# Two turned loads of w2 placed one unit earlier in the first pass of a fused backward kernel

## The chip, the cores and the metric

The kernel runs on one core of one Trainium2 chip, as one program. The metric is the device time of one execution in microseconds (us); lower is better. A profiled execution gives the trace: every instruction with its engine, line, start and duration, the DMA packets, and who released whom. TensorE (PE) multiplies matrices, with its weight loads shown apart (PEld), VectorE is DVE, ScalarE is ACT, GpSimd is POOL and SyncE is SP; the last two mostly issue DMAs here.

## The reference

The reference computes a gated sum of two branches and all its gradients. Cut to what matters:

```python
def forward(x, w_r, w_i, w1, b1, w2, b2, gate_w, B_x):    # x: 1 x 2048 x 1024
    g = sigmoid((x * gate_w).sum(-1, keepdims=True))
    a = irfft2(rfft2(x) * (w_r + 1j * w_i))               # spectral branch
    h = relu(x @ w1 + b1) ** 2                            # w1: 1024 x 3584
    b = h @ w2 + b2                                       # w2: 3584 x 1024
    return g * a + (1 - g) * b

out, vjp = jax.vjp(forward, ...)
return out, *vjp(grad_out)      # gradients of x, w_r, w_i, w1, b1, w2, b2, gate_w
```

`x` is the argument `A_x`; both branches read it. Inputs and outputs are bfloat16.

## The kernel before, in words

The work has three passes over the dense branch, with the spectral branch (the "side") dealt into their gaps.

The first pass, `mlp_in`, makes the hidden layer and its gradient. The 3584 hidden columns are 28 chunks of 128, taken in 14 pairs `fp`; two pairs make one of seven groups `fg` of 512 columns, the first being group 0. After a start over pairs 0 and 1, the pass is a list of units `(fp, sp)`, where `sp` is a half of the 2048 rows: (2,0), (2,1), (3,0), (3,1), (4,0), (4,1) and so on up to pair 10, then five more in another order. A unit makes the hidden layer of its pair and half with seven products (`p1` to `p7`, matmuls of L876, each a chain of four of 512 columns) and, in between, the four gradient products of the unit before it (`back_(waiting[0..3])`, matmuls of L776, chains of eight), each closed by a VectorE instruction (L780) that writes `dhT`; `later["last"]` is the newest of these. A unit takes some 16 us.

The gradient products read `w2T`, a group of w2 turned by the DMA itself: `load_w2(fg)` issues two transposing DMAs on SyncE (L183 is the helper), each of 256 rows of w2, half a megabyte. The tile `w2T` has two buffers, so group `fg + 1` is written over group `fg - 1`. A unit's gradient products belong to the unit before it, so the last products of group `fg - 1` run in the first unit of group `fg`. The load is tied to `later["last"]`: SyncE waits for that instruction before it issues.

Also on SyncE are the loads of w1 (`w1g`, L798, half a megabyte for each pair, two buffers), which `load_w1(fp + 1)` asks for at the start of a pair's first unit. The side's first stage, `first_stage`, takes 16 pairs of row tiles `src`, eight of x and then eight of the incoming gradient. GpSimd issues their loads (L707) from the fourth pair on, into three buffers; VectorE folds each pair (`uv`, L273 and L274, then L278 to L285), ScalarE copies edges of the folds (L280 to L286), TensorE transforms them (L294, L326), and GpSimd stores the result to `z_scr` (L240).

The order of instructions on each engine is chosen by a planner, which goes by the order of the text where it can, by expected durations, and by explicit ties: `after(...)` with its default is a real wait, with `NoSync` an order on one engine only. Each engine then runs its own list strictly in order. The same holds for SyncE and GpSimd as issuers of DMAs.

Of the kernel before, what the change touches and what calls it, by code (L numbers as in the profile page):

```python
# [141 lines left out]
def kernel(  # L142
# [35 lines left out]
    FGW, FG, FGC = g.FGW, g.FG, g.FGC  # L178
# [557 lines left out]
    def mlp_in():  # L736
# [48 lines left out]
        def load_w2(fg, earlier=None):  # L785

            w2T[fg] = wb.tile([P, DC, FGW], BF16, name="w2T", tag="w2T", bufs=2)
            for h in (0, FGW // 2):
                f0 = fg * FGW + h
                after(turned(w2T[fg][:, :, h : h + FGW // 2], B_w2[f0 : f0 + FGW // 2, :]), earlier)  # L790
# [5 lines left out]
        def load_w1(fp):  # L796
            w1[fp] = f1.tile([P, DC, PW], BF16, name="w1f", tag="w1f") if fp == 2 else wb.tile([P, DC, PW], BF16, name="w1g", tag="w1g", bufs=2)
            ld(out=w1[fp][:], in_=w1v[:, :, fp * PW : (fp + 1) * PW])  # L798
# [27 lines left out]
        def back_(fp, s, c):  # L826
            if (fp, s // 2) not in dh:
                dh[fp, s // 2], left_of[fp, s // 2] = wide("dhT"), 4
            last = grads(2 * fp + c, s, rows_(s), rTs.pop((fp, s, c)), dh[fp, s // 2][:, c, rows_(s % 2)])
            later["last"] = last  # L830
            left_of[fp, s // 2] -= 1
            if not left_of[fp, s // 2]:
                store(dhT_scr, dh.pop((fp, s // 2)), fp, s // 2)
# [23 lines left out]
        def w_sums(fp, tie=None):  # L857
            (a11, a12), (a21, a22) = w_quads(fp)
            if fp % 2:
                s_ = kept[:, NT - 2 : NT, :].rearrange("p t (n f) -> p (t n) f", f=P).rearrange("p (q n) f -> p q n f", q=4)  # L860
            else:
                s_ = wb.tile([P, 4, KH, P], FP16, name="Sw", tag="Sw", bufs=1)
            s1, s2, s3, s4 = (s_[:, n] for n in range(4))
            for out, x, y, op in ((s1, a21, a22, ALU.add), (s2, s1, a11, ALU.subtract), (s3, a11, a21, ALU.subtract), (s4, a12, s2, ALU.subtract)):
                after(V(out=out, in0=x, in1=y, op=op), later["last"] if tie else None, mybir.DependencyClass.NoSync)
                yield
            S_[fp] = {1: s1, 2: s2, 3: s3, 4: s4}
# [67 lines left out]
        def sum_of_db(n):  # L935
            ec, h = divmod(n, 2)
            summed = nc.vector.reduce_sum(out=gb2[:, ec, h : h + 1], in_=dbT[:, ec, h * S // 2 : (h + 1) * S // 2], axis=mybir.AxisListType.X)
            after(summed, later["last"], mybir.DependencyClass.NoSync)

        def grad_of_b2():  # L940
            whole = wb.tile([P, DC], BF16, name="gb2b", tag="gb2b")
            V(out=whole[:], in0=gb2[:, :, 0], in1=gb2[:, :, 1], op=ALU.add)
            pb = fps.tile([DC, P], BF16, name="pb2", tag="ps2", bufs=2)
            nc.tensor.transpose(pb[:], whole[:], identb[:])
            row = wb.tile([DC, P], BF16, name="gb2r", tag="gb2r")
            nc.vector.tensor_copy(out=row[:], in_=pb[:])
            st(out=out_7.rearrange("(c p) -> c p", p=P), in_=row[:])
# [27 lines left out]
        def freed_rows(n, low, high):  # L975
            if n == freed + 1:
                again(slice(2 * low, 2 * low + 2), later["last"])
            elif n == len(seq) - 1 and high:
                again(slice(6 + 2 * high, 8 + 2 * high))
# [4 lines left out]
        for n, u in enumerate(units_):  # L984
            fg, pr = divmod(u.fp, NPR)
            if (u.fp, u.sp) == (LAST - 2, 1):
                load_w1(LAST)
            elif u.sp == 0 and u.fp < LAST - 1:
                load_w1(u.fp + 1)
            u.p1()  # L990
            if n:
                units_[n - 1].square(0, u.copy)
            back_(*waiting[0])
            u.p5()
            freed_rows(n, 0, 1)
            if first and u.sp and "mid" in later and u.fp >= FC // 4:
                turned_group(0, *first.pop(0), later["last"])
            yield
            next(more_sums, None)
            u.p6()  # L1000
            freed_rows(n, 1, 2)
            if n:
                units_[n - 1].square(1, u.copy)
            back_(*waiting[1])
            next(more_sums, None)
            follows = u.fp + 1 if u.sp == 1 and u.fp < LAST - 2 else {(LAST - 2, 0): LAST - 1, (LAST - 1, 1): LAST}.get((u.fp, u.sp))
            ahead_ = w_sums(follows, True) if follows else iter(())
            dealt = ahead_ if (u.fp, u.sp) != (LAST - 2, 0) else iter(())
            next(dealt, None)
            yield  # L1010
            u.p7()
            back_(*waiting[2])
            next(more_sums, None)
            next(dealt, None)
            freed_rows(n, 2, 0)
            yield
            back_(*waiting[3])
            for _ in ahead_:
                pass
            next(more_sums, None)  # L1020
            if pr == 0 and u.sp == 0:
                later["blocks"] = later["last"]
            if 0 < fg < FG - 1 and pr == 0 and u.sp:
                load_w2(fg + 1, later["last"])
            if 0 < n <= 2 * DC:
                sum_of_db(n - 1)
            elif n == 2 * DC + 1:
                grad_of_b2()
            u.p4()
            freed_rows(n, 3, 3)  # L1030
            u.p3()
            if n + 1 < len(units_):
                units_[n + 1].p2()
            yield
            waiting = [(u.fp, 2 * u.sp + j, c) for c, j in ((0, 0), (0, 1), (1, 1), (1, 0))]
# [17 lines left out]
    def turned_group(n, i, k, earlier):  # L1053
        scr, fg = (h2T_scr, dhT_scr)[n // FG], n % FG
        rows_ = scr[:].rearrange("c p s -> (c p) s")[fg * FGW + i * FGW // 2 : fg * FGW + (i + 1) * FGW // 2]
        tiles, f_ = slice(k * NT // 2, (k + 1) * NT // 2), slice(i * FGW // 2, (i + 1) * FGW // 2)
        after(turned(group(n)[:, tiles, f_], rows_[:, k * S // 2 : (k + 1) * S // 2]), earlier)
# [699 lines left out]
    warm(7)  # L1757

    units = mlp_in()
    rows_of_x(0)  # L1760
    vrow = f1.tile([FC + DC, P], BF16, name="vrow", tag="vrow")
# [136 lines left out]
```

## Time and profile before

| what | value |
|---|---|
| median of three runs | 1201.8 us (1199.36 to 1203.73) |
| the profiled execution | 1199.23 us, of which span 1197.5 us |
| TensorE busy | 1179.0 us, 98% of the span |
| VectorE, ScalarE, GpSimd busy | 889.6, 533.2, 375.4 us |
| granted TensorE clock | 1.00 |
| DMA moved | 249.84 MB, mean 209 GB/s |
| first pass | from the start to about 460 us |
| w2 groups three to seven, first issue | 110.9, 177.3, 241.1, 303.4 and 364.8 us |

The span runs from the first to the last instruction of the program; the execution's own time has about 1.7 us more around it. Busy time is the union of an engine's instructions. Matmuls are pipelined and their ends are modelled, so a busy TensorE can still lose a little time between starts. An idle stretch is put down to the semaphore that came last.

### The profile page before, as it was taken

To read this page: it belongs to the slowest core of one execution; us is meant where nothing else is said; L and a number is where in the kernel's file an instruction comes from. 1 tells how busy PE (TensorE), PEld (TensorE's weight loads), DVE (VectorE), ACT (ScalarE), POOL (GpSimd) and SP (SyncE) were. 2 spreads that over 40 slices of the span, in tenths; PEclk is the share of its full clock that TensorE was granted. 3 is DMA by queue.
4 is the path that set the end of the run, shared out by engine and by line. 5 is a ranking of instruction groups with operands and counts; after the bars stand their busy time and mean duration, and the time that the engine had idled before them with its cause. 6 is when DMAs were issued, how large, how long until landed. Compare 5 with 4: busy or idle time off the path is not lost.

```text
span 1197.5 us, 19460 instructions
## 1 busy us (share of the span) xinstructions
PE 1179.0 (98%) x7201; PEld 635.5 (53%) x7295; DVE 889.6 (74%) x1593; ACT 533.2 (45%) x959; POOL 375.4 (31%) x618
## 2 busy tenths in 40 slices
PE   9999999999999999999999999999999999999998
PEld 5555555443333444444446899999544444444444
DVE  4898886688988888767638656566786677986757
ACT  4678787576767773444415556554201010000000
POOL 0233443566666663643322322321001100000000
PEclk9999999999999999999999999999999999999999
DMA  9996757796969888989897999995879999665530
GB/s 289 266 309 172 225 168 189 207 223 185 223 177 200 251 242 180 200 188 215 201 225 155 224 226 236 254 202 157 262 184 264 244 276 263 184 190 153 179 124 36
DMA packets 329465, 249.84 MB, mean 209 GB/s; under 512 B 187913, under 2 KB 287659, under 8 KB 328859
## 3 DMA queue, kind: packets, MB, share of 16 engines
q1 hardware_dynamic: 268352, 112.12, 44.0%
q0 software_dynamic: 35136, 111.72, 29.2%
q10 hardware_dynamic: 25882, 24.76, 7.2%
q8 instruction: 57, 0.93, 0.3%
q14 instruction: 38, 0.30, 0.1%
HBM read 114.82 MB, written 89.67 MB: 171 GB/s over the span
## 4 chain that ended last, share of the span: by engine, by line
PE 66%; DVE 10%; ACT 3%; issue 3%; ACTq 0%; POOL 0%; DMA 0%; DVEq 0%; POOLq 0%
PE pX L1194 16%; PE xX L1493 14%; PE pV L1194 12%; PE xV L1493 7%; PE pd L776 5%; PE ph L876 4%; PE xZ L1493 4%; PE pui L326 1%; PE pki L592 1%; PE px L436 1%; DVE rT L892 1%; DVE dhT L780 1%; PE pv L467 1%; DVE tt L447 1%; DVE oT L1441 1%
## 5 line engine op out<-in xcount | busy, mean ns | idle before, releaser
L776 PE MATMUL pd<-dbT,w2T 128*128 128x512 bf16 x861 | 205.8, 379 | 2.2 <-DVE dhT L780 0.4
L776 PEld LDWEIGHTS <-w2T 128*128 128x128 bf16 x896 | 86.5, 98 | 104.1 <-issue 4.3
L1493 PEld LDWEIGHTS <-dS 128*128 128x128 f16 x686 | 66.4, 98 | 78.6 <-issue 3.0
L780 DVE SCALAR_TENSOR_TENSOR dhT<-pd,rT 128x512 bf16<-128x512 f32 x112 | 76.5, 683 | 27.0 <-PE pd L776 23.6
L1544 POOL DMA_DIRECT2D out_dram<-ot x32 | 17.4, 542 | 250.7 <-DVE ot L1600 128.0
L1610 ACT ACTIVATE w2br<-w2br,dsc 128x512 f32<-128x512 bf16 x8 | 5.8, 722 | 175.8 <-DVE ot L1600 117.4
L1210 ACT COPY u<-pX 128x512 f32<-128x512 f32 x56 | 32.8, 585 | 98.7 <-PE pX L1194 93.3
L1493 PE MATMUL xX<-oT,dS 128*128 128x512 f16 x336 | 76.4, 379 | 0.2 <-DVE eR L1522 0.2
L1493 PEld LDWEIGHTS <-odd 128*128 128x128 bf16 (+1 forms) x462 | 44.8, 98 | 51.5 <-issue 0.9
L1493 PEld LDWEIGHTS <-even 128*128 128x128 bf16 (+1 forms) x448 | 43.7, 98 | 52.6 <-issue 0.7
L1194 PEld LDWEIGHTS <-T 128*128 128x128 f16 x672 | 64.7, 98 | 7.8 <-issue 0.7
L893 ACT ACTIVATE rT<-rT 128x512 bf16<-128x512 bf16 x69 | 43.3, 628 | 42.8 <-DVE rT L892 42.8
L761 ACT ACTIVATE h2T<-rT 128x1024 bf16<-128x1024 bf16 x56 | 59.6, 1065 | 0.5 <-issue 0.2
L1214 DVE TENSOR_TENSOR whi<-pV,u 128x512 bf16<-128x512 f32 x28 | 19.3, 688 | 51.6 <-ACT u L1210 51.5
L476 POOL DMA_DIRECT2D y_scr<-pc x64 | 46.9, 734 | 34.1 <-DVE pc L473 31.6
L447 DVE TENSOR_TENSOR tt<-x,w 128x1028 f16<-128x1028 f16 (+1 forms) x64 | 42.0, 690 | 17.1 <-issue 12.6
L1194 PEld LDWEIGHTS <-S 128*128 128x128 f16 x336 | 32.3, 98 | 41.0 <-DVE S L1126 1.3
L1194 PEld LDWEIGHTS <-resL 128*128 128x128 bf16 x448 | 43.0, 98 | 4.7
L1194 PEld LDWEIGHTS <-resR 128*128 128x128 f16 (+1 forms) x448 | 42.9, 98 | 4.9 <-issue 0.2
L807 POOL DMA_DIRECT2D h2T_scr<-h2T x28 | 20.7, 738 | 74.0 <-ACT h2T L761 54.1
L1194 PEld LDWEIGHTS <-even 128*128 128x128 bf16 (+1 forms) x256 | 24.5, 98 | 30.8 <-issue 2.1
L500 POOL DMA_DIRECT2D out_dram<-gw x64 | 34.4, 542 | 19.4 <-ACT gw L496 13.9
(383 smaller groups left out, 2748.3 us busy)
## 6 DMA issues: line engine op xcount, KB each, us to landing
h2T_scr<-h2T POOLq DMA_DIRECT2D x28, 512.0 KB, 4.1
dhT_scr<-dhT POOLq DMA_DIRECT2D x28, 512.0 KB, 4.7
y_scr<-pc POOLq DMA_DIRECT2D x64, 128.0 KB, 3.8
ax_scr<-yo POOLq DMA_DIRECT2D x16, 512.0 KB, 5.0
out_dram<-ot POOLq DMA_DIRECT2D x31, 256.0 KB, 3.4
z<-z_scr ACTq DMA_DIRECT2D x60, 128.0 KB, 4.1
out_dram<-whi POOLq DMA_DIRECT2D x28, 256.0 KB, 5.3
out_dram<-wlo POOLq DMA_DIRECT2D x28, 256.0 KB, 4.7
```

Of the source, the lines that this page charges most:

```text
L447: V(out=tt[:, k, :, :, 0:W], in0=x[:, a : a + 2, :, 0:W], in1=by, op=ALU.mult)
L476: st(out=columns_of(y_scr, c, h), in_=pc[:, n])
L500: st(out=every(dst_w, k), in_=gw[lanes[n], c_, 0:W1])
L761: after(nc.scalar.activation(h2T, rT, ACT.Square), behind_, mybir.DependencyClass.NoSync)
L776: mm(pd[:], lhsT=w_[:, ec, fc % FGC * P : (fc % FGC + 1) * P], rhs=dbT[:, ec, ss], start=(ec == 0), stop=(ec == DC - 1),)
L780: return STT(out=dhT, in0=pd[:], scalar=2.0, in1=rT, op0=ALU.mult, op1=ALU.mult, accum_out=gb1part[:, fc, sb : sb + 1],)
L807: st(out=scr[2 * fp : 2 * fp + 2, :, cols2].rearrange("c p s -> p c s"), in_=t_[:])
L876: mm(acc[:], lhsT=lhs[:, t, :], rhs=rhs[:, t, :], start=start and t == 0, stop=t == KH - 1, skip_group_check=True)
L893: nc.scalar.activation(rT, rT, ACT.Relu)
L1194: self.mm = mm(out, lhsT=lhs[:, t, m * P : (m + 1) * P], rhs=rhs[:, t, :], start=start and t + a == 0, stop=t == KH - 1, skip_group_check= ...
L1210: turn["ACT"] = nc.scalar.copy(out=t_[:], in_=self.X[:])
L1493: ins = mm(acc, lhsT=lhs[:, fc, :], rhs=rhs[:, fc, :], start=start and fc == 0, stop=fc == KH - 1 and bias is None, skip_group_check=True,)
```

## The change

For each group from the second on, the load of the next group is asked for after the last gradient product of the first pair's unit. Before, this was the second unit of that pair (`u.sp` is 1) for all groups. Now it is the first unit (`u.sp` is 0) where `fg` is 1 or 2, so for the loads of the third and fourth group (`load_w2(2)` and `load_w2(3)`), and still the second unit where `fg` is 3, 4 or 5.

```diff
             if pr == 0 and u.sp == 0:
                 later["blocks"] = later["last"]
-            if 0 < fg < FG - 1 and pr == 0 and u.sp:
+            if 0 < fg < FG - 1 and pr == 0 and u.sp == (fg > 2):
                 load_w2(fg + 1, later["last"])
```

In units of the list, the third group's load moves from (2,1) to (2,0), and the fourth's from (4,1) to (4,0). No instruction is added or removed.

## The prediction

> **What bounds the kernel.** I read the page's busy times first, then its chain of work that ended last, then stretches of the first pass, then the queues around the two loads that move.
>
> ```profile
> span 1197.5 us, 19460 instructions
> PE 1179.0 (98%) x7201; PEld 635.5 (53%) x7295; DVE 889.6 (74%) x1593; ACT 533.2 (45%) x959; POOL 375.4 (31%) x618
> PE 66%; DVE 10%; ACT 3%; issue 3%; ACTq 0%; POOL 0%; DMA 0%; DVEq 0%; POOLq 0%
> ```
>
> TensorE (PE) is busy for 1179.0 of 1197.5 us, so all its idle time is 18.5 us, start and end included; the chain that ended last is mostly matmuls, and DMA has 0% of it. An edit that moves loads can only win back idle TensorE time, or add some. Where that lies near the moved loads is seen by stretches (columns: us; PE, PEld, DVE, ACT, POOL busy with counts; granted clock; DMA share; GB/s):
>
> ```profile
> 90.00:107.50 17.50, 17.10 (x117) 9.27 (x117) 15.54 (x32) 14.20 (x30) 7.78 (x14) 1.00 0.48 161
> 107.50:125.00 17.50, 17.28 (x127) 9.90 (x127) 13.78 (x30) 14.43 (x30) 7.09 (x14) 1.00 0.91 225
> 157.50:172.50 15.00, 14.89 (x109) 8.59 (x110) 12.83 (x31) 12.42 (x25) 5.88 (x12) 1.00 0.41 131
> 172.50:190.00 17.50, 17.39 (x120) 9.74 (x121) 14.35 (x32) 15.19 (x32) 6.95 (x14) 1.00 1.00 208
> 190.00:207.50 17.50, 15.97 (x112) 8.83 (x112) 10.39 (x23) 12.81 (x26) 4.52 (x8) 1.00 0.59 176
> ```
>
> The clock is 1.00 throughout. Today's loads fall into 107.5 to 125 (DMA 0.91) and 172.5 to 190 (DMA 1.00); the stretches where they will fall are at 0.48 and 0.41. TensorE idles little except after the second load: 17.50 - 15.97 = 1.53 us in 190 to 207.5. SyncE's queue shows the loads (start, time to issue):
>
> ```profile
> 110.89 9.63 SPq L183 DMA_TRANSPOSE w2T<-in_B_w_dram  x2
> 144.05 0.37 SPq L798 DMA_DIRECT2D w1g<-in_B_w_dram  x1
> 177.31 7.40 SPq L183 DMA_TRANSPOSE w2T<-in_B_w_dram  x2
> 184.82 26.85 SPq L798 DMA_DIRECT2D w1g<-in_B_w_dram  x2
> ```
>
> Why TensorE idles after the second load stands in the time lines of VectorE (DVE), ScalarE (ACT) and TensorE; the bracket is the idle time before the instruction and what ended it:
>
> ```profile
> 191.51 0.48 DVE L723 TENSOR_SCALAR kg<-kf,gcol 128x256 f16<-128x256 f16 x2
> 194.57 0.69 DVE L273 TENSOR_TENSOR uv<-src 128x1024 f16<-128x1024 bf16 x1 [2.58 <-DMA src<-in_grad_out_dram]
> 195.90 0.21 ACT L280 COPY f<-uv 128x4 f16<-128x4 f16 x1 [2.21 <-DVE uv L274]
> 196.73 1.02 PE L876 MATMUL ph<-xT,w1g 128*128 128x512 bf16 x4 [0.68 <-ACT rT L890]
> 200.32 1.02 PE L876 MATMUL ph<-dbn 128*128 128x512 f16 x4 [0.58 <-DVE rT L892]
> ```
>
> The last pair of gradient rows (src) landed late. VectorE, which works in order, stood 2.58 us before the fold that reads it; ScalarE stood behind the fold, with the relu that empties a PSUM bank queued after it; TensorE then wanted that bank. The src pair was issued by GpSimd at 180.56 and 181.14, in the middle of the transposes, and took 11.7 and 13.3 us to land; the same pair issued at 159.7, with no transposes in flight, took 3.0 and 3.8, one issued at 112.7, under the earlier transposes, 7.0.
>
> **The two loads leave their places.** Nothing waits for w2 itself: the idle time before its products is put down to VectorE or the weight load's issue, never to a w2 DMA. Group three is in flight from 110.89 and landed by 123.4, while its first product runs at 163.9; group four's first product runs near 228.5. So 38 us or more are spare already, and a sooner start wins nothing by being sooner. [...]
>
> What is worth something is what they collide with. Leaving 177.3 to about 190 frees the src pair of 180.56: with a delay of 3.0 to 7.0 us it lands by 188.2, and VectorE could start the fold at 191.51 + 0.48 = 191.99. The 2.58 us wait goes whole. For TensorE that is 0.68 + 0.10 + 0.58 + 0.06 = 1.4 us of idle gaps (two more small ones in the same stretch). Modelled ends hide a little: matmuls of 512 columns start 216 ns apart here, and counted by starts those four places lose 0.79 + 0.26 + 0.75 + 0.23 = 2.0 us. I take 2.0, as starts are recorded and ends are modelled; ends 1.4 and, if all of VectorE's wait reached the end, 2.6. Leaving 110.89 wins 0: the pair under it still landed at 120.3, 5.1 us before its fold at 125.42.
>
> **The two loads arrive elsewhere.** Each is released by the last gradient product of its unit (L780). Group three then goes at 94.78 + 0.68, so 95.5, group four at 160.69 + 0.68, so 161.4: 15.4 and 15.9 us sooner. Both still take the buffer whose last reader is that same product, so no new wait arises, but no slack is left. On SyncE nothing stands between old and new place (72.78's two w1 loads are out by 77.5; 144.05's by 144.4), so neither load passes another there. What is behind them moves up: the w1 load of 184.82 needed only the end of the unit, about 178.1, and goes some 6.6 us sooner, against src pairs issued near it. The nearest row is the src pair of 142.43 with a w1 load at 144.05: landed in 4.0. Cost 0, cover as above: 191.99 against 185.2.
>
> At the new place group four meets the src pair issued at 159.72 and 160.26, folded at 171.68. At 7.0 us that lands by 167.3; at 13.3, by 173.6, 1.9 us late. Group three meets the pair of 93.36 and 93.91, folded at 105.36: by 100.9, or 107.2 and 1.9 late. Price by VectorE's row: 2.0 of TensorE for 2.58, so at most 1.5 each. I take 0 for both, since the pairs are issued 1 to 2 us ahead of the transposes and DMA is at 0.41 and 0.48 there; the pair of 112.7, issued 1.8 us behind transposes, is the nearer row. [...]
>
> **What cannot be read.** The order on each engine is not that of the text: the w1 loads of the fourth and fifth pair of chunks leave together from 72.78, ahead of group three's transposes, though the text has the second of them after. The order is planned with expected landings, so two loads moved by 16 us may rearrange what follows. The trace has no row for that. Bounds: idle TensorE time from 75 to 450, summed over 25 us stretches, is 7.5 us, so the gain ends near 8; the loss is bounded by more waits of the size just priced, four of them 8.0 less the 2.0 won. I take 0 for the sum.
>
> **Sum.** 1199.23 us (1197.5 span and 1.7 around it) less 2.0 is 1197.2 for the profiled execution. That one lies 2.6 below the median of the three runs, 1201.8, so the median goes to 1199.8. A measurement of this kernel tells about 0.3%, 3.6 us, from no change; the three runs themselves lie 4.4 apart.
>
> **The rivals.**
>
> Re-planned, closer: the stall goes and about half of the other 6.0 us of idle time in 75 to 450 closes too, -5.0, so 1196.8 (1193.8 to 1198.2). For it: side work runs 2.6 us sooner from 194 on, and the DMA peaks at 0.91 and 1.00 are both flattened. Against: no single row of those 6.0 us is over 1.1.
>
> Slower: the new order sets folds of src pairs at the heads of VectorE's and ScalarE's queues before the pairs land. Place: the seven gradient pairs before the last, which land only 4.0 to 9.5 us ahead of their folds. Price 2.0 each, less the 2.0 won; two cost +2.0 and stay within the measurement, from three (+4.0) it is slower. I take four, +6.0, 1207.8. Against it: none of the seven waits today, and DMA at the new places is under half busy.
>
> Hidden or undone: the planner keeps the loads late, or the src pair is late from what else is queued around 180 to 190 (z_scr and h2T stores, the w1 load). Then 1201.8. Against: SyncE is free at both new times.
>
> **How the numbers follow.** Forecast 0.35, its own range 1197.2 to 1202.4 (the 1.4 to 2.6, and half the scatter of the runs): of it 0.09 beyond 0.3% faster, 0.26 within. Closer 0.29, all faster. Slower 0.31: 0.30 beyond, 0.01 within. Hidden 0.05: 0.03 within, 0.01 each side. Faster 0.39, within 0.30, slower 0.31. Both signs hold much of the chance, as a re-planned order is the largest unknown. The range 1194.5 to 1208.0 leaves out the deepest part of the second case and more than four waits.
>
> **What would show it.** Right: transposes at about 95.5 and 161.4; DMA share in 172.5 to 190 well below 1.00; the last src pair landing in 7 us or less and no DMA wait before the fold at L273; TensorE idle in 190 to 207.5 down from 1.53 to 0.3. Wrong: a DMA wait at L273 for the pairs issued near 93 or 160; or the instructions of TensorE and VectorE in another order between 75 and 450, with idle time in places that today have none.

## The result, and the profile after

| | before | changed |
|---|---|---|
| median of 8 runs each | 1201.63 us (1199.36 to 1205.79) | 1196.68 us (1196.18 to 1199.39) |
| profiled execution, and its span | 1199.23, 1197.5 us | 1196.72, 1195.0 us |

The ratio is 0.9959, 95% interval 0.9944 to 0.9974: faster by 4.95 us in the medians, 0.4%. The forecast of 1199.8 had the sign. The measured median lies 3.1 us below it, 0.5 us outside the forecast's own range (1197.2 to 1202.4) and inside the full one (1194.5 to 1208.0); the gain was two and a half times the 2.0 us of its sum. Two things are to be explained: that it is faster, and why by 5 us when the two profiled executions lie 2.5 apart.

The top of the page after:

```profile
span 1195.0 us, 19460 instructions
PE 1178.1 (99%) x7201; PEld 634.4 (53%) x7295; DVE 889.9 (74%) x1593; ACT 533.5 (45%) x959; POOL 375.5 (31%) x618
```

TensorE does the same work and its idle time is 16.9 us where it was 18.5. The same stretches as before (us; PE, PEld, DVE, ACT, POOL busy; granted clock; DMA share; GB/s):

```profile
90.00:107.50 17.50, 17.11 (x117) 9.30 (x118) 15.50 (x32) 14.38 (x30) 7.23 (x13) 1.00 0.84 213
107.50:125.00 17.50, 17.28 (x120) 9.61 (x121) 13.78 (x31) 14.32 (x31) 7.09 (x14) 1.00 0.53 181
157.50:172.50 15.00, 14.89 (x110) 8.59 (x111) 12.68 (x31) 12.41 (x26) 5.33 (x11) 1.00 0.88 175
172.50:190.00 17.50, 17.39 (x121) 9.68 (x122) 14.91 (x33) 15.19 (x32) 6.95 (x14) 1.00 0.75 246
190.00:207.50 17.50, 17.39 (x121) 9.77 (x122) 11.38 (x26) 14.66 (x29) 5.53 (x11) 1.00 0.47 138
```

The DMA work changed places (0.48 to 0.84 and 0.91 to 0.53 for the third group, 0.41 to 0.88 and 1.00 to 0.75 for the fourth), and only one TensorE figure moved: 15.97 became 17.39 in 190 to 207.5. SyncE's queue:

```profile
96.05 8.41 SPq L183 DMA_TRANSPOSE w2T<-in_B_w_dram  x2
144.60 0.37 SPq L798 DMA_DIRECT2D w1g<-in_B_w_dram  x1
161.96 10.94 SPq L183 DMA_TRANSPOSE w2T<-in_B_w_dram  x2
177.99 32.17 SPq L798 DMA_DIRECT2D w1g<-in_B_w_dram  x2
```

Both loads start where the forecast put them (95.5 and 161.4; this execution runs 0.55 us late from its first matmuls on), and the w1 load behind them goes at 178.0 in place of 184.8. The last pair of gradient rows (the duration of its issue in ns, then the time to landing), and VectorE's fold that reads it:

```profile
L707 POOL DMA_DIRECT2D src<-in_grad_out_dram x2: 554/568/583, 181.1 to 181.7; - x2
DMA to landing us min/median/max: 6.1/6.1/6.2
```

```profile
192.06 0.48 DVE L723 TENSOR_SCALAR kg<-kf,gcol 128x256 f16<-128x256 f16 x2
192.46 0.69 DVE L273 TENSOR_TENSOR uv<-src 128x1024 f16<-128x1024 bf16 x1
```

The pair lands in 6.1 us, where it took 11.7 and 13.3, and the fold follows with no bracket behind it: the 2.58 us wait is gone.

The order of the instructions is the same before and after on all five engines, so the traces can be laid on one another weight load by weight load. The changed kernel runs 0.55 us behind up to the fold. Between 196 and 204 it wins 2.1 us, in four places: 0.84, 0.26, 0.75 and 0.23 by the starts of the weight loads, the same four that the prediction had counted. It keeps that lead to 384, and wins another 1.0 us where the profile before has a 1.07 us gap at 386, behind a late z load. That makes 2.5. The gap at 386 is in none of the five further profiles of the kernel before (below), so it was an accident of that execution, and the change's own part of the 2.5 is 2.1.

### The profile page after: what moved, and what is told of

The parts are those of the page before. It is cut to its first block, busy times and chain, and to the rows that moved or that the text cites. A ratio compares the mean times of both kernels' runs of the same rounds, so it can differ in the third digit from the quotient of the medians.

```text
span 1195.0 us, 19460 instructions
## 1 busy us (share of the span) xinstructions
PE 1178.1 (99%) x7201; PEld 634.4 (53%) x7295; DVE 889.9 (74%) x1593; ACT 533.5 (45%) x959; POOL 375.5 (31%) x618
## 4 chain that ended last, share of the span: by engine, by line
PE 83%; DVE 10%; ACT 3%; issue 3%; DMA 1%; ACTq 0%; SPq 0%; DVEq 0%
PE pX L1194 16%; PE xX L1493 14%; PE pd L776 12%; PE pV L1194 12%; PE ph L876 7%; PE xV L1493 7%; PE xZ L1493 4%; PE ph L769 2%; PE pui L326 1%; PE px L436 1%; PE pki L592 1%; PE pZ L876 1%; PE pv L467 1%; PE pu L326 1%; PE pk L294 1%
## 5 line engine op out<-in xcount | busy, mean ns | idle before, releaser
L447 DVE TENSOR_TENSOR tt<-x,w 128x1028 f16<-128x1028 f16 (+1 forms) x64 | 42.0, 691 | 18.5 <-issue 12.6
L411 POOL COPY w<-wn 128x512 bf16<-128x512 bf16 x32 | 20.8, 649 | 63.5 <-DVE tt L447 62.3
```

What stands on the lines that cost most here:

```text
L447: V(out=tt[:, k, :, :, 0:W], in0=x[:, a : a + 2, :, 0:W], in1=by, op=ALU.mult)
```

## The experiments

Two theories stood at the outset. A: the whole gain is the fourth load's collision with the last src pair. B: every load that leaves a full stretch of DMA is worth something, so both moves share the gain. When the first results were in, a third question came up, why the median gains more than the profile shows. The experiments ran on three chips, each beside runs of the kernel before on the same chip, whose medians there were 1201.71, 1202.14 and 1204.78 us; each ratio compares runs on one chip.

**Only the third group's load sooner.**

```diff
-            if 0 < fg < FG - 1 and pr == 0 and u.sp:
+            if 0 < fg < FG - 1 and pr == 0 and u.sp == (fg > 1):
```

> Only the third group's load goes one unit sooner (about 95.5 us in place of 110.9); the fourth stays at 177. Theory A (the whole gain is the fourth load no longer colliding with the last pair of gradient rows): no change, 1201.6 us within 1.5, the fold of the last src pair still waits 2 us or more for its DMA. Theory B (each load that leaves a stretch in which the DMA engines are full is worth something): about half of the gain, 1199.

Measured 1201.16 us against 1201.71, ratio 1.0005 (0.9989 to 1.0021): nothing, as A has it. B is out for this load. Its profile brought something that no theory had. The wait at the fold (us in all, times, longest), TensorE's time line, and three stretches around it:

```profile
DVE uv L273 <- DMA src<-in_grad_out_dram: 3.9, 1, 3.9
```

```profile
198.05 1.49 PE L876 MATMUL ph<-xT,w1g 128*128 128x512 bf16 x4 [1.99 <-ACT rT L890]
199.34 3.15 PE L776 MATMUL pd<-dbT,w2T 128*128 128x512 bf16 x8
```

```profile
195.40:198.50 3.10, 1.11 (x12) 0.74 (x11) 2.58 (x5) 0.79 (x2) 0.00 (x0) 0.99 1.14 323
198.50:201.90 3.40, 3.40 (x10) 1.21 (x9) 3.40 (x9) 2.29 (x7) 0.91 (x2) 0.50 0.80 311
201.90:205.30 3.40, 3.40 (x28) 2.06 (x28) 1.62 (x5) 3.37 (x5) 1.75 (x3) 1.00 0.51 122
```

Here the src pair took 14.5 us, VectorE stood 3.9 us and TensorE 1.99. Then the granted clock fell to 0.50 for 3.4 us: eight gradient matmuls that take 1.89 us elsewhere took 3.15. Laid on the changed kernel's trace, this place costs 3.8 us: 2.1 in the gap and 1.7 in the half clock (half of 3.4). The half clock in turn hides the three smaller losses that the first profile has behind its first gap (0.26, 0.75 and 0.23, so 1.2 us), as the slower matmuls give VectorE time; its net price here is some 0.4 us.

**Only the fourth group's load sooner.**

```diff
-            if 0 < fg < FG - 1 and pr == 0 and u.sp:
+            if 0 < fg < FG - 1 and pr == 0 and u.sp == (fg != 2):
```

> Only the fourth group's load goes one unit sooner (about 161 us in place of 177); the third stays at 110.9. Theory A: the whole gain, 1196.7 us, the last src pair lands within 7 us and TensorE's idle time in 190 to 207.5 us is 0.1 to 0.3. Theory B: about half of the gain, 1199.

Measured 1197.08 us, ratio 0.9974 (0.9957 to 0.9991). The pair lands in 6.0 us, and the stretch reads as in the changed kernel:

```profile
190.00:207.50 17.50, 17.39 (x121) 9.74 (x121) 12.16 (x27) 14.22 (x28) 5.53 (x11) 1.00 0.42 121
```

In the medians 4.6 of the 4.95 us are there with this move alone. The ratio, which sets runs beside runs, gives 3.1 us (1.1 to 5.2); its interval overlaps the change's. With the first experiment's zero, the gain, or most of it, belongs to the fourth load.

**The src pair sooner, w2 left alone.** One more pair is asked for in the step that asks for the pair before it.

```diff
-                    ahead_to(j + 2, later["last"])
+                    ahead_to(j + (3 if j == NT - 4 else 2), later["last"])
```

> w2's loads stay where they were; in their stead the last pair of gradient rows is asked for together with the pair before it, about 7 us sooner, ahead of the transposes. Theory A: no wait at the fold, 1196.7 us. Theory B: no gain, 1201.6 us, as the transposes are where they were.

Measured 1197.00 us, ratio 0.9975 (0.9959 to 0.9991), with the transposes still issued at 177.5 and the orders on TensorE, VectorE, ScalarE and SyncE as before. The two pairs, issued together from 173.2, took at most 6.2 us, and TensorE's idle time is gone although the DMA stays busier than after the change:

```profile
DMA to landing us min/median/max: 5.0/6.0/6.2
```

```profile
190.00:207.50 17.50, 17.39 (x121) 9.76 (x122) 11.77 (x27) 14.27 (x28) 5.52 (x12) 1.00 0.59 189
```

So no w2 load need move for the gain, which is 4.7 us by the medians and 3.0 (1.1 to 4.9) by the ratio. This is the plainest proof of A: the victim was taken out of the way in place of the culprit, and the wait and TensorE's idle time went just as well.

One part of the culprit is not separated. A w1 load is queued behind the transposes, and it goes 7 us sooner when they leave. In the nine profiles where the third group's load stands at 110.9 with no w1 load near, the pair issued at 113 behind it took 7.0 to 8.3 us; in the five where that load had moved, 3.3 to 4.4. The last pair took 5.4 to 6.2 us beside a w1 load alone, and 11.1 to 14.6 with both. That points to a share of both loads in the late landing; no run moves the w1 load alone.

**The fourth group's load later.**

```diff
-            if 0 < fg < FG - 1 and pr == 0 and u.sp:
+            if 0 < fg < FG - 1 and (pr, u.sp) == ((1, 0) if fg == 2 else (0, 1)):
```

> The fourth group's load goes one unit later in place of sooner (about 197 us, first product at 228), the third stays. Theory A: it is out of the last src pair's way just as well, so 1196.7 us and no wait at the fold, although the load has 16 us less to spare. Theory B, and any account by which an earlier load is what counts: no gain or slower, 1201.6 us or more.

Measured 1198.16 us, ratio 0.9988 (0.9964 to 1.0011), so by time alone it is unclear; three of its 12 runs lie at 1203.8 to 1207.0, with a mean granted clock of 0.997 to 0.999 where the other nine have 1.000. What they met isn't known, as the profile is of another run. The profile agrees with A as to the place: the load goes at 195.6, the pair lands in 5.8 us or less, and 190 to 207.5 is whole again:

```profile
190.00:207.50 17.50, 17.39 (x120) 9.74 (x121) 11.53 (x26) 14.51 (x29) 5.53 (x11) 1.00 0.70 194
```

What this execution wins there it loses in the third pass, where TensorE stands for a block load; the stretch around it has the clock whole:

```profile
951.16 2.97 PE L1493 MATMUL xX<-w2left,odd 128*128 128x512 bf16 x13 [1.98 <-DMA odd<-h2T_scr]
```

```profile
940.00:960.00 20.00, 18.02 (x82) 7.74 (x82) 11.83 (x21) 1.06 (x1) 2.68 (x5) 1.00 0.95 256
```

That wait came in the first experiment's profile too (1.94 us) and once in the changed kernel's own (1.7 us, below), and in none of the six profiles of the kernel before. It may be scatter that the change does not touch; so few profiles do not show that.

**All groups sooner.**

```diff
-            if 0 < fg < FG - 1 and pr == 0 and u.sp:
+            if 0 < fg < FG - 1 and pr == 0 and u.sp == 0:
```

> All groups' loads from the third to the seventh go one unit sooner. Theory A: the later groups meet no src pair, since the last one is folded by 200 us; so their move adds nothing by that route, 1196.7 us like the change. Rival: the later loads meet the side's z loads and turned blocks at their new places and cost 1 to 3 us there (1198 to 1200), which would be why they are better left.

Measured 1205.69 us against 1202.14, ratio 1.0023 (0.9999 to 1.0047). It has the gain at the fold (no wait there, clock 1.00) and gives it back: the rival was right, with a price of some 9 us against the change's median (measured on another chip) and not 1 to 3. The fifth group's load now goes at 223.4, some 3 us ahead of two z tiles that ScalarE asks for at 226.5 and 227.0. The first of them took 8.4 us to land, against 3.0 in the changed kernel. VectorE waits for them (us in all, times, longest), TensorE waits for VectorE, and the clock falls:

```profile
DVE pm L426 <- DMA z<-z_scr: 5.1, 1, 5.1
```

```profile
239.07 2.80 PE L776 MATMUL pd<-dbT,w2T 128*128 128x512 bf16 x7 [2.98 <-DVE dhT L780]
241.67 1.84 PE L876 MATMUL ph<-dbn,w1g 128*128 128x512 f16 x4
```

```profile
235.70:239.90 4.20, 1.16 (x7) 0.48 (x5) 1.92 (x6) 0.00 (x0) 0.00 (x0) 1.00 0.56 156
239.90:243.30 3.40, 3.40 (x9) 1.22 (x8) 2.00 (x5) 2.69 (x5) 0.00 (x0) 0.50 0.13 39
```

A gap of 2.98 us, then again 3.4 us at half clock: laid on the changed kernel's trace, 5.2 us are lost between 234 and 246, and another 2.0 in the third pass between 924 and 950. This execution took 1203.59 us; what the longer ones met isn't shown.

**All but the fifth sooner.**

```diff
-            if 0 < fg < FG - 1 and pr == 0 and u.sp:
+            if 0 < fg < FG - 1 and pr == 0 and u.sp == (fg == 3):
```

> The loads of groups three, four, six and seven go one unit sooner, the fifth stays (that one met the side's z loads). If the fifth's move is the whole cost of moving all, this lies at the change's 1196.7 us or up to 0.7 below it, with no half clock between 200 and 400 us. Rival: the sixth and seventh cost something too, and it lies at 1198 or more.

Measured 1196.83 us against 1204.78 of before on that chip, ratio 0.9935 (0.9914 to 0.9955), clock 1.00 between 200 and 400. The fifth load's move is all that sets this version apart from the one with all groups sooner, so it was the whole cost of moving all, as far as medians from two chips (1205.69 and 1196.83) tell. It is no clear gain over the change itself, which ran beside it:

> The change once more on this chip, beside the version with groups three, four, six and seven sooner: 1196.7 us, no wait at the last fold, clock 1.00 throughout, times within 3 us of each other.

The change again: 1197.89 us, ratio 0.9939 (0.992 to 0.9958). No wait at the fold, clock 1.00. Its profiled run, at 1199.23, is the longest of the six, for TensorE waited for two block loads:

```profile
PE xX L1493 <- DMA odd<-h2T_scr: 1.7, 1, 1.7
PE xX L1493 <- DMA even<-h2T_scr: 0.6, 1, 0.6
```

**The kernel before, five more profiles,** to see how its wait scatters.

> The kernel before once more, for another sample of its wait. Theory A with a clock term: the last src pair's landing scatters from run to run; where TensorE stands 2 us or more, the granted clock falls to half for some 3.4 us behind it, and the time lies at 1201 us or more; where TensorE stands under 1.5 us, the clock stays at 1.00 and the time lies below 1200. Rival: the wait is always that of the first profile (2.6 us at the fold, 1.4 of TensorE) and the scatter of the times comes from elsewhere, such as block loads in the third pass.

> As for the other repeat of the kernel before: the time, the wait at the last fold and the half clock go together (clock term), or do not (rival).

> As for the other two repeats of the kernel before: the time, the wait at the last fold and the half clock go together (clock term), or do not (rival).

> The kernel before, a fifth profile. Clock term: if this run lies at 1201 us or more, its fold waits 3.5 us or more and the granted clock is 0.5 for about 3.4 us near 198 us; if it lies below 1200, the wait is under 3 us and the clock stays at 1.00.

> The kernel before, a sixth profile. As for the fifth: at 1201 us or more the wait at the fold is 3.5 us or more and the clock falls to 0.5 near 198 us; below 1200 neither is seen.

With the first profile, and the first experiment's, whose fourth load stands at the same place (before a to e, in the order of the five texts; cost: what TensorE loses between 196 and 204 against the changed kernel, by the starts of the same weight loads):

| profile | time, us | VectorE's wait at the fold, us | TensorE's first gap, before L876, us | clock behind it | cost, us |
|---|---|---|---|---|---|
| before b | 1197.61 | 1.3 | none | 1.00 | 0.8 |
| before a | 1197.99 | 1.9 | none | 1.00 | 1.4 |
| before c | 1198.81 | 2.5 | 0.62 | 1.00 | 2.0 |
| before d | 1198.84 | 2.5 | 0.62 | 1.00 | 2.0 |
| before, the first | 1199.23 | 2.6 | 0.68 | 1.00 | 2.1 |
| before e | 1199.55 | 3.3 | 1.45 | 1.00 | 2.8 |
| third group only | 1201.85 | 3.9 | 1.99 | 0.50 for 3.4 us | 3.8 |

The wait is there in every profile of before, and it is never the same: 1.3 to 3.3 us. Its cost is the wait less some 0.5 us, and in the last row, where the clock falls, the wait less 0.1. Profile e, with the longest wait of the six, has the same two lines as above with the clock still whole:

```profile
198.00 1.02 PE L876 MATMUL ph<-xT,w1g 128*128 128x512 bf16 x4 [1.45 <-ACT rT L890]
199.12 1.89 PE L776 MATMUL pd<-dbT,w2T 128*128 128x512 bf16 x8
```

The part of the expectation for runs under 1200 us held in all five. The part for 1201 us and more was not met by any, because none of these five got so long. That matters: 46 of the 71 timed runs of the kernel before, beside these kernels, lie at 1201 us or more, above all six of its profiles. A longer wait at the fold is the account that fits, since two separate ways of taking it away, the load moved sooner and the pair moved sooner, bring the times to 1197 and narrow them. But the largest cost seen, 3.8 us, added to the change's 1196.7 gives 1200.5, some 1 us short of the median before, and no profile shows a run of 1202 or of 1209.4.

The mean granted clock, which is listed for 63 of these 71 runs, tells more. A profile with one drop, 3.4 us at half clock, has a mean of 0.999 (half of 3.4 in 1200 us is 0.0014). Of the 41 runs at 1201 us or more, 31 have a mean below 1.000, down to 0.995, which by this estimate is three or four drops; of the 22 shorter runs, 3 do. Of the 44 runs of the change and of three other versions (fourth alone sooner, src pair sooner, all but the fifth), 5 have a mean below 1.000, and one lies at 1201 us or more; of the 12 with the fourth load later, 3 and 4. So a lowered clock goes with most of the long runs of the kernel before. Ten of them, up to 1204.2 us, have the clock at 1.000, and the largest cost seen with the clock whole is 2.8 us. How long the wait at the fold is in the long runs, where in the run their clock falls, and what made those ten long, stays open.

## Why the prediction was right, and where its sum was off

The mechanism was read rightly from before. The late src pair was the cause, through VectorE's and ScalarE's queues in order (the fourth load alone, and the src pair sooner, each bring the gain). Leaving 110.9 was worth 0, as put (the third load alone). Both loads start at the computed times with no new wait. The pairs at the new places keep their spare time: the one beside the fourth load landed at 164.8, against 167.3 allowed and 171.7 needed; the one beside the third at 97.9, against 100.9 and 105.4. The w1 load moved up to 178.0 as worked out, and the last pair landed at 187.9, not 185.2, still 4.6 us ahead of its fold. (The load issued at 159.7, which the prediction calls the same pair, is an earlier pair.) Idle time in 190 to 207.5 is 0.11 us, where 0.3 was named.

The step that was mis-sized is the 2.0 us of the sum. For the execution that it was read from it is right: laid on the changed kernel's trace, that place costs 2.1. But it was priced from this one execution, with the note that it lies 2.6 us below the median, and then carried over to the median as if the wait were a constant. It is not: 1.3 to 3.9 us in seven profiles, with the cost going from 0.8 to 3.8 beside it, and in the longest of them a second term sets in, the half clock, which the sum didn't have at all (1.7 us gross, some 0.4 net). What the median has beyond that execution, 2.4 us, was never looked into, and no profile shows it whole. The bounds named for the term, 1.4 to 2.6, were bounds of one execution's bookkeeping and not of the wait.

The half clock followed TensorE gaps of 1.99 us (third group only) and 2.98 (all groups sooner), and did not follow those of 1.45 (before e), 1.7 (the change again), 1.94 (third group only, in the third pass) and 1.98 (fourth later). The length of a gap alone does not tell, as 1.98 and 1.99 went different ways.

Both large rivals, a closer order and one with more waits, rested on a re-planned order. The order came out the same on every engine, so neither came about, and 0.60 of the chances hung on something that did not happen. That faster came out anyway was not their merit: it was the forecast's case with a larger price. The closer order's number, 1196.8, was met to 0.1 us by luck. The unread risk lay elsewhere: moving a load may meet another small load that is due soon, as the fifth group's did, for some 9 us; the prediction named that for src pairs alone.

## What to carry to other kernels

A big load that nobody waits for can still be what costs time, by what else is in flight: look up who issues small loads with a near deadline while it runs, and move either of the two. Before moving a load into a quiet stretch, list the small loads due there too; moved by one unit each, the fourth load won 3 to 5 us and the fifth lost some 9. And a stall that depends on landing times is a spread, not a number: price it from several profiles, or from the distance between the shortest and the median run, look at the mean clock of every run, and allow for a half clock where TensorE may stand as long as it did ahead of the drops here, 1.99 and 2.98 us.

## What the runs showed of the hardware that was not expected

A TensorE gap of 1.99 us, in a stretch of 3.1 us with 1.11 us busy, was followed by a granted clock of 0.50 for 3.4 us; so was one of 2.98 us (0.50 for 3.4 us, with all groups sooner). Gaps of 1.45, 1.7, 1.94 and 1.98 us were not. What tells 1.98 from 1.99 is not shown. The 4.2 us around the second gap have 1.16 us busy; in profile e the same 3.1 us as in the first have 1.65, and the clock stayed at 1.00.

A quarter-megabyte load by GpSimd, which lands in 3.0 to 3.8 us when issued at 159.7 with no transposes in flight, took 7.0 to 8.3 us when issued some 2 us behind the start of a megabyte of transposing DMAs (group three's, which in the kernel before took 12.5 us from first issue to last landing, 110.89 to 123.4), 5.4 to 6.2 us beside a w1 load alone, and 11.1 to 14.6 us when issued some 3 us behind the transposes and ahead of a w1 load. Issued ahead of the transposes, by 1.1 to 1.7 us, at 160.3 and 160.8 in the changed kernel, it took 3.2 to 4.0 us.
